# Loading the first column piece of w_down as two halves

## The chip, the core and the metric

The kernel runs on one core of a Trainium2 chip. It computes one decode step of a transformer block: conditioned layer norm, cached grouped-query attention over 65,536 positions, then a gated feed-forward layer. The metric is the device time of one execution in microseconds (us), of which lower is better. A profile is one execution taken by the hardware profiler; its span is about 1.4 us shorter than the timed figure of the same execution (437.0 against 438.43 us for the kernel before).

The engines are PE (TensorE, matmul; PEld is its weight load), DVE (VectorE), ACT (ScalarE), POOL (GpSimd), and SP, which here only issues DMAs.

## The reference, cut to what matters

The change touches only the very last product, the multiplication by `w_down` (3584 x 1024, bf16), and the sum with the residual:

```python
def _B_ref(x, w_gate, w_up, w_down):
    return _gelu(x @ w_gate) * (x @ w_up) @ w_down
...
h = _layernorm(x, axis=-1) * (1 + cb) + sb
x = x + gb * _B_ref(h, B_w_gate, B_w_up, B_w_down)
return x
```

There is one token, so every weight matrix is read once and used for a matrix-vector product. `w_down` is 7.3 MB of the 185.6 MB that the kernel reads from HBM.

## The kernel before

`w_down` is cut into seven blocks of 1 MB, numbered b = 0 to 6. A block holds four rows per partition (`UE = 4`), of 1024 columns (`D`). Blocks 0 to 4 are the row part, blocks 5 and 6 the column part.

```python
NBF = FD // UE          # 7
b = 0
NROW = NBF - 2          # 5: blocks 5 and 6 are multiplied column-wise
while b + 2 < NROW:     # blocks 0+1 and 2+3: 2 MB each
    ...
while b < NBF:
    for e, ne in ((0, UE),) if b + 1 < NBF else ((0, 2), (2, 1), (3, 1)):
        if b == NROW:   # block 5: beside block 4, in the same buffer
            jb = plan_load(
                wd_v[:, b, e:e + ne, :], flat(ne, D), jb.slot, beside=jb, off=UE * D, sem=9)
        else:
            jb = plan_load(wd_v[:, b, e:e + ne, :], flat(ne, D), next(tail_d))
        j_d.append((jb, jb.view, b * UE + e, ne))
    b += 1
```

So the last loads, in order, are 1 MB (block 4, the row piece), 1 MB (block 5), 512 KB, 256 KB and 256 KB (block 6). All go out on one queue; each has a semaphore that PE waits for.

The row part is multiplied with the activation as the stationary operand and the weights streaming past, and leaves partial sums along the rows of PSUM (`kt_ps` in the views). They must be turned into a column and added to the column part. The turn is two DVE transposes (L860), followed by eight small matmuls on PE, which I call the fold (L868; the program's four float32 matmuls show as eight). The column part takes the weights as the stationary operand, 128 columns at a time, with one activation column moving (L386): eight matmuls for each row of a block, so 32 for a block of 1 MB.

```python
early = [a for a in j_d if a[2] < NROW * UE]
v = row_matvec(place_d, early, o_pad, (v_uc,), (NQ - 1, NROW * UE - NQ))     # L409
DVE.wait(v)
for h in range(2):
    v_rows = DVE.done(dve.transpose(...))                                     # L860
late = j_d[len(early):]
col_matvec(acc_dn, late[:1], o_pad[:, :, 0], KD, True)                        # L386
PE.wait(v_rows, v_sel)
turned = row_a.rearrange("p (a k r) -> p a k r", a=NQ, r=QD)
for a in range(NQ):
    pe.matmul(acc_dn[QD * a:QD * (a + 1), :], sel32[:, :], turned[:, a, :, 0],
              start=False, stop=True, skip_group_check=True)                  # L868, the fold
v = col_matvec(acc_dn, late[1:], o_pad[:, :, 0], KD, False)                   # L386
DVE.wait(v)
v = DVE.done(dve.tensor_tensor(t_dn, acc_dn, mod_sb[:, 5, :], ALU.mult))      # L873
DVE.wait(v)
v = DVE.done(dve.tensor_tensor(y_col, t_dn, x1_col[:, :], ALU.add))           # L875
SP.wait(v)
sp.dma_start(out[0, 0].rearrange("(p k) -> p k", p=P), y_col)...              # L877
```

`late` is the list of column pieces. `late[:1]` is its first piece and `late[1:]` the rest. The fold stands between them, so the meaning of "first piece" decides where the fold stands. `col_matvec` waits for each piece's own semaphore in turn.

## Time and profile before

| Kernel before | |
|---|---|
| time | 438.57 us median (438.42 to 438.61, 6 runs) |
| span of the profiled execution | 437.0 us |
| read from HBM | 185.60 MB, 425 GB/s over the span |

The first view is the page's own slices, 40 equal ones over the span. The DMA line is the busy share in tenths, and the line under it is what the DMA engines moved.

```profile
DMA  8999999999999999999999999999999999999995
GB/s 359 432 425 441 433 430 427 439 425 438 435 432 432 433 432 432 432 435 432 432 438 432 432 433 432 432 432 432 432 432 432 432 427 435 439 432 433 420 422 229
```

The body of the kernel is a stream of loads that keeps the DMA engines at 8 or 9 tenths in every slice but the last, so I read its time as set by bytes. Only the last slice shows the DMA engines half idle: there the stream is over, and something else still runs. The next view is the chain of waits of the kernel before, in order of time: start, duration, what.

```profile
398.61 32.14 DMA slots<-in_B_w_down_dram
430.76 0.05 issue
430.80 2.09 PE b L386 x32
432.89 0.22 PE b L868 x8
433.11 2.03 PE b L386 x32
435.15 0.02 issue
435.17 0.18 DVE kt_sb L873
```

From 430.80 to 435.15 us the chain is PE work with no gap. The timeline of the same kernel tells what preceded it (start, duration, engine, line, operation; in brackets the idle time of the engine before it and what ended it).

```profile
428.35 1.05 PE L409 MATMUL kt_ps<-slots,p_row 128*32 128x512 bf16 x8 [0.51 <-DMA slots<-in_B_w_down_dram]
429.47 1.31 DVE L860 STREAM_TRANSPOSE kt_sb<-kt_ps 128x512 f32<-128x512 f32 x2 [7.69 <-PE kt_ps L409]
430.80 2.09 PE L386 MATMUL b<-p_row,slots 128*128 128x1 bf16 x32 [1.40 <-DMA slots<-in_B_w_down_dram]
432.82 0.29 PE L868 MATMUL b<-kt_sb,sel 128*32 128x8 f32 x8
433.05 2.09 PE L386 MATMUL b<-p_row,slots 128*128 128x1 bf16 x32
435.17 0.17 DVE L873 TENSOR_TENSOR kt_sb<-b,mod_sb 128x8 f32<-128x8 f32 x1 [4.39 <-PE b L386]
```

PE finishes the row part at 429.40 and then sits idle for 1.40 us until all of block 5 has landed. The second group of 32 follows the fold without a gap, so the pieces of block 6 were there in time.

A DMA's semaphore is counted up in 16 steps, and a load has landed at the last of them. Read so from the trace, in us from the span's start:

```
                 block 4   block 5   512 KB   256 KB   256 KB
kernel before     428.30    430.76   432.05   432.70   433.29
```

The data is complete at 433.29, but the last DVE product starts only at 435.17. PE is late because it began late.

### The profile page before, as it was taken

The page shows a single profiled execution, that of the slowest core. Times are in us where ns is not written, and L with a number is a line of the kernel's source. Part 1 is how long each engine was busy: PE and PEld are TensorE (multiplying, and loading weights), DVE is VectorE, ACT ScalarE, POOL GpSimd, SP SyncE. Part 2 cuts the span into 40 slices and gives each one's busy share as a digit, 9 for nine tenths or more (in the row PEclk, how much of TensorE's full clock was granted, in tenths as well). Part 3 has the DMA queues.
Part 4 walks back from the last instruction along what each step waited for, and adds up shares of the span by engine and source line. Part 5 has one row for each costly group of instructions (what it writes and reads, how often), then busy time and mean ns, then how long its engine had stood idle before and what let it go on. Part 6 is the DMA issues. An engine that isn't in the chain of part 4 may idle for free.

```text
span 437.0 us, 8422 instructions
## 1 busy us (share of the span) xinstructions
PE 306.8 (70%) x3858; PEld 201.2 (46%) x3858; DVE 206.7 (47%) x303; ACT 111.3 (25%) x164; POOL 16.8 (4%) x23
## 2 busy tenths in 40 slices
PE   0435459969697778959687895969778596575356
PEld 0112236646565555636465563646556363232024
DVE  6601014646474656737373763737476365321001
ACT  1000001533333513433241353333235334000000
POOL 9500000000000000000000000000000000000000
PEclk9986669988798978979696897879889879578685
DMA  8999999999999999999999999999999999999995
GB/s 359 432 425 441 433 430 427 439 425 438 435 432 432 433 432 432 432 435 432 432 438 432 432 433 432 432 432 432 432 432 432 432 427 435 439 432 433 420 422 229
DMA packets 8048, 185.77 MB, mean 425 GB/s; under 512 B 994, under 2 KB 994, under 8 KB 1380
## 3 DMA queue, kind: packets, MB, share of 16 engines
q1 hardware_dynamic: 8032, 185.60, 98.8%
q8 instruction: 8, 0.13, 0.1%
q14 instruction: 4, 0.03, 0.0%
q10 hardware_dynamic: 4, 0.00, 0.0%
HBM read 185.60 MB, written 0.00 MB: 425 GB/s over the span
## 4 chain that ended last, share of the span: by engine, by line
DMA 55%; PE 32%; DVE 10%; issue 1%; ACT 1%; POOL 0%; SPq 0%; POOLq 0%
DMA slots<-in_A_k_cache_dram 44%; PE kt_ps L575 16%; DMA slots<-in_B_w_down_dram 7%; PE b L645 5%; PE sc_ps L597 4%; DMA slots<-in_A_v_cache_dram 4%; PE kt_ps L409 4%; DVE selt L359 3%; DVE kt_sb L683 2%; DVE s_pad L717 1%; DVE o_red L706 1%; PE b L386 1%; PE sc_ps L626 1%; PE b L613 1%; DVE o_acc L694 1%
## 5 line engine op out<-in xcount | busy, mean ns | idle before, releaser
L575 PE MATMUL kt_ps<-ident,slots 128*128 128x128 bf16 x2048 | 157.6, 238 | 45.5 <-DMA slots<-in_A_k_cache_dram 44.7
L575 PEld LDWEIGHTS kt_ps<-ident,slots 128*128 128x128 bf16 x2048 | 136.9, 108 | 71.8 <-issue 41.0
L683 DVE COPY kt_sb<-kt_ps 128x2048 bf16<-128x2048 bf16 x96 | 117.6, 1225 | 109.5 <-PE kt_ps L575 107.8
L683 ACT ACTIVATE kt_sb<-kt_ps 128x2048 bf16<-128x2048 bf16 x32 | 60.1, 1878 | 28.0 <-PE kt_ps L575 28.0
L732 ACT ACTIVATE p_sb<-sc_ps 128x512 bf16<-128x512 bf16 x32 | 19.1, 598 | 181.6 <-PE sc_ps L626 181.6
L597 PE MATMUL sc_ps<-kt_sb,q_buf 128*32 128x512 bf16 x528 | 51.9, 428 | 0.0
L645 PE MATMUL b<-slots,p_sb 128*32 128x512 bf16 x560 | 42.0, 427 | 4.6 <-DMA slots<-in_A_v_cache_dram 3.9
L409 PE MATMUL kt_ps<-slots,h_pad 128*32 128x512 bf16 x176 | 19.4, 579 | 21.9 <-DMA slots<-in_A_wq_dram 9.5
L694 DVE SCALAR_TENSOR_TENSOR o_acc<-o_acc,s_pad,b 128x512 f32<-128x512 f32 x28 | 20.9, 747 | 13.5 <-PE b L645 13.4
L613 PE MATMUL b<-m_sp,selt 128*128 128x16 f32 x66 | 13.0, 272 | 18.1 <-DVE m_sp L722 16.5
L645 PEld LDWEIGHTS b<-slots,p_sb 128*32 128x32 bf16 x560 | 16.1, 108 | 20.7 <-issue 7.5
L717 DVE TENSOR_REDUCE s_pad<-sc_ps 128x1 f32<-128x512 f32 x32 | 21.8, 681 | 0.0
L738 ACT ACTIVATE p_row<-sc_ps,s_pad 128x512 bf16<-128x512 f32 x32 | 21.7, 678 | 0.0
L409 PEld LDWEIGHTS kt_ps<-slots,h_pad 128*32 128x32 bf16 x176 | 6.4, 129 | 32.7 <-issue 11.4
L613 PEld LDWEIGHTS b<-m_sp,selt 128*128 128x128 f32 x66 | 9.8, 188 | 23.7 <-DVE m_sp L722 21.3
L597 PEld LDWEIGHTS sc_ps<-kt_sb,q_buf 128*32 128x32 bf16 x528 | 11.0, 95 | 12.4 <-issue 4.7
L409 PE MATMUL kt_ps<-slots,s_pad 128*32 128x512 bf16 x96 | 11.6, 543 | 6.6 <-DMA slots<-in_w_mod_dram 6.6
L452 POOL TENSOR_TENSOR rs<-va,halfneg 128x1 f32<-128x1 f32 x2 | 1.1, 557 | 376.4 <-DVE va L449 376.4
L793 DVE COPY kt_sb<-kt_ps 128x512 f32<-128x512 f32 x3 | 2.1, 692 | 27.4 <-PE kt_ps L409 27.4
L626 PEld LDWEIGHTS sc_ps<-ident,p_row 128*128 128x128 bf16 x136 | 7.8, 99 | 15.1 <-issue 14.4
L626 PE MATMUL sc_ps<-ident,p_row 128*128 128x128 bf16 x136 | 13.7, 224 | 0.2 <-ACT p_row L738 0.2
L409 PE MATMUL kt_ps<-slots,p_row 128*32 128x512 bf16 x104 | 10.0, 543 | 4.4 <-DMA slots<-in_B_w_down_dram 3.6
(98 smaller groups left out, 142.8 us busy)
## 6 DMA issues: line engine op xcount, KB each, us to landing
slots<-in_A_k_cache_dram SPq DMA_DIRECT2D x16, 4096.0 KB, 23.1
slots<-in_A_v_cache_dram SPq DMA_DIRECT2D x16, 4096.0 KB, 23.2
slots<-in_w_mod_dram SPq DMA_DIRECT2D x4, 3072.0 KB, 20.3
slots<-in_A_wq_dram SPq DMA_DIRECT2D x2, 4096.0 KB, 35.3
slots<-in_A_wo_dram SPq DMA_DIRECT2D x4, 2048.0 KB, 24.6
slots<-in_B_w_gate_dram SPq DMA_DIRECT2D x2, 3584.0 KB, 29.5
slots<-in_B_w_up_dram SPq DMA_DIRECT2D x2, 3584.0 KB, 29.5
slots<-in_B_w_down_dram SPq DMA_DIRECT2D x2, 2048.0 KB, 34.4
```

The source lines that it names most:

```text
L359: dve.tensor_scalar(selt[:, :].rearrange("p (r h) -> p r h", h=REP), selw[:, HQ - REP:HQ].unsqueeze(1).to_broadcast([P, NR, REP]), -scale, ...
L409: ins = pe.matmul(out, pad[:, k, :], view[:, kk, c0:c0 + ROW], start=k <= last_k[0], stop=k >= last_k[1], skip_group_check=True,)
L575: ins = pe.transpose(kt_ps[:, half * 2048 + t * P:half * 2048 + (t + 1) * P], j_k[i - i % KU].view[:, i % KU * CH + b * TB + t, :], ident[ ...
L597: ins = pe.matmul(sc(j)[QD * g:QD * (g + 1), :], q_buf[:, j % SITES, QD * b:QD * (b + 1)], kt_sb[:, j % 2, n:n + w, :].rearrange("p n d -> ...
L613: ins = pe.matmul(b6[:, 0:NR], selt[:, :], m_sp[:, j % 2, :], start=True, stop=True)
L626: ins = pe.transpose(sc_bf[:, o:o + P], p_row[:, j % 2, c * P:(c + 1) * P], ident[:, :])
L645: ins = pe.matmul(b7[QD * c:QD * (c + 1), :].rearrange("p (b d) -> p b d", b=NB), p_sb[:, s, c * P + QD * g:c * P + QD * (g + 1)], v[:, NQ ...
L683: ev[i % SITES][b].done(act.activation(dst, src, ACT.Copy) if E_ is AC else dve.tensor_copy(dst, src))
L694: v = oc[j % SITES].done(dve.scalar_tensor_tensor(o_acc[:, :], o_acc[:, :], al[:, j:j + 1], b7[:, :], ALU.mult, ALU.add))
L717: v = DVE.done(dve.tensor_reduce(m_new, sc(j), AX.X, ALU.max))
L732: pc[jt % SITES].done(act.activation(p_sb[:, jt % SITES, :], sc_bf[:, o:o + ROW], ACT.Copy))
L738: v_x[j] = ex[s].done(act.activation(p_row[:, j % 2, :], sc(j), ACT.Exp, bias=mneg[:, j:j + 1], scale=scale, accum_out=zr[:, j:j + 1],))
```

## The change

The intent is to let PE start on block 5 when half of it is there. Each half gets a semaphore of its own (numbers 9 and 7), so that PE can wait for each half alone.

```diff
-            for e, ne in ((0, UE),) if b + 1 < NBF else ((0, 2), (2, 1), (3, 1)):
+            for e, ne in ((0, UE),) if b < NROW else ((0, 2), (2, 2)) if b == NROW else ((0, 2), (2, 1), (3, 1)):
                 if b == NROW:
                     jb = plan_load(
-                        wd_v[:, b, e:e + ne, :], flat(ne, D), jb.slot, beside=jb, off=UE * D, sem=9)
+                        wd_v[:, b, e:e + ne, :], flat(ne, D), jb.slot, beside=jb, off=(UE + e) * D, sem=9 - e)
```

Because `late[:1]` is now a half, the fold moves as well: PE's order is 16 column matmuls, fold, 48 column matmuls, in place of 32, fold, 32. No other instruction moves.

## The prediction

> **What bounds the kernel now.** The span is 437.0 us. The slices of the page show the DMA engines at 8 to 9 tenths nearly throughout, mostly at 432 GB/s, with 185.6 MB read: the body is a stream of loads, and the change leaves its bytes alone. What it can move is the tail. The chain of waits ends: DMA of w_down until 430.76; column matvec 2.09 us (32 matmuls); fold of the turned rows 0.22 us (L868); column matvec 2.03 us (32 matmuls, from 433.11); two DVE steps of 0.18 us; then the output store, issued at 435.57.
>
> By the semaphore updates in the trace, the last loads land at 428.30 (the piece before), 430.76 (the 1 MB piece), 432.05 (512 KB), 432.70 and 433.29 (256 KB each). PE idles 1.40 us for the 1 MB piece, and the remaining 4.4 us are PE work, though the last byte lands at 433.29 and needs only 8 matmuls, 60 ns apart.
>
> **What the change does.** It splits the 1 MB load into two of 512 KB, each waited for on its own. The fold now stands after the first half: 16 column matmuls, fold, 16, then 32, instead of 32, fold, 32. Matmuls and bytes are the same; one DMA issue (0.43 us on SP, far ahead of the data) and one semaphore wait are added.
>
> **Costs.** In this stream a 512 KB piece landed 1.29 us after its predecessor, where half of the 1 MB step would be 1.23 us. I estimate the first half to land at 429.55 to 429.6, the second near 430.85; later pieces shift by up to 0.1 us. The Trainium skill, "DMA: Bandwidth & Descriptors", section "Rules for kernel authors", advises at least 1 MiB per DMA for bandwidth; the 1.29 us (406 GB/s) of this trace says that the loss is small when loads are queued behind one another.
>
> **The critical path after.** PE starts at 429.6 and does 16 matmuls by 430.65. The fold needs the DVE transposes, which end at 430.78, so it starts near 430.83: a new wait of 0.1 to 0.2 us on DVE. Then 16 matmuls from 431.05 to 432.05, about when the 512 KB piece of the last block lands (432.1). From there 32 matmuls, 2.13 us to the DVE step as before (433.04 to 435.17): DVE starts near 434.25 rather than 435.17. The gain is about 0.9 of the 1.2 us by which the first half comes sooner; DVE and the 512 KB landing take the rest. The stream before 428 is untouched.
>
> Predicted time: 438.57 - 0.9 = 437.65 us, 8 in 10 between 437.0 and 438.4 (run-to-run scatter 0.2 us, some drift between chips). Faster by over 2%: 0.01; within 2%: 0.98; slower by over 2%: 0.01.
>
> **What would show it.** PE's idle time before the first column matmuls, put down to DMA, falls from 1.40 us to about 0.2. The fold is preceded by a wait on the DVE transpose (L860). The column matvecs run from 429.6 to 434.2. The last landing stays within 0.1 us of 433.29. The idle time before the DVE product L873 ends about 0.9 us sooner. The chain of waits turns to DVE L860 or the last 512 KB landing.
>
> **What would make it wrong.** Smaller pieces that cost the stream more than 0.1 us; landings of the halves bunched together, since the 16 engines finish one load over 1.85 us and the slowest sets its landing; a granted clock other than the 0.5 of this tail; SP blocked on a full queue (its last two issues took 5.7 and 6.6 us) for long enough to starve it.

## The result, and the profile after

| | before | after |
|---|---|---|
| time, median (range) of 6 runs each | 438.57 us (438.42 to 438.61) | 437.56 us (437.46 to 437.69) |
| ratio | | 0.9978, 95% interval 0.9965 to 0.9990 |
| span of the profiled execution | 437.0 us | 436.2 us |
| start of the DVE product L873 | 435.17 | 434.32 |

The ratio and its interval are given as recorded, from fast runs alone; the ratio of the medians quoted would be 0.9977. The change gains 1.01 us by the medians, 0.2% of the whole. The ranges of the two kernels do not overlap, though by a limit of 2% the two count as the same.

The chain of waits after the change, in order of time:

```profile
397.44 30.93 DMA slots<-in_B_w_down_dram
428.38 0.04 issue
428.42 1.10 PE kt_ps L409 x8
429.52 0.03 issue
429.55 1.33 DVE kt_sb L860 x2
430.87 0.04 issue
430.92 0.29 PE b L868 x8
431.21 3.09 PE b L386 x48
434.30 0.02 issue
434.32 0.18 DVE kt_sb L873
```

The load that the chain hangs on is now block 4, landing at 428.38, and no longer block 5. Between it and PE's last stretch stand the row matmuls and the DVE transposes. The timeline after the change shows the former idle time in use:

```profile
429.55 1.31 DVE L860 STREAM_TRANSPOSE kt_sb<-kt_ps 128x512 f32<-128x512 f32 x2 [6.81 <-PE kt_ps L409]
429.67 1.13 PE L386 MATMUL b<-p_row,slots 128*128 128x1 bf16 x16 [0.19 <-DMA slots<-in_B_w_down_dram]
430.91 0.20 PEld L868 LDWEIGHTS b<-kt_sb,sel 128*32 128x32 f32 x8 [0.20 <-DVE kt_sb L860]
430.92 0.29 PE L868 MATMUL b<-kt_sb,sel 128*32 128x8 f32 x8
431.14 3.14 PE L386 MATMUL b<-p_row,slots 128*128 128x1 bf16 x48
434.32 0.17 DVE L873 TENSOR_TENSOR kt_sb<-b,mod_sb 128x8 f32<-128x8 f32 x1 [3.46 <-PE b L386]
```

PE's wait of 1.40 us for block 5 has become 0.19 us for its first half and 0.20 us (on the weight load) for the transposes. Sixteen column matmuls run while DVE transposes. After the fold there are 48, not 32, but they start at 431.14 rather than 433.05.

The landings after the change:

```
                 block 4   1st half   2nd half   512 KB   256 KB   256 KB
kernel after      428.38     429.62     430.89   432.13   432.76   433.40
```

The last byte lands 4.99 us after block 4 before the change (433.29 - 428.30) and 5.02 us after it now (433.40 - 428.38). The extra DMA cost the stream about 0.03 us. The rest of the shift, 0.08 us, was there when block 4 landed, ahead of anything that the change touched on the queue; the profiled executions below scatter by about 0.3 us at that point. I therefore compare profiles by the time from the landing of block 4 to the start of the DVE product. It is 6.87 us before (435.17 - 428.30) and 5.94 us after (434.32 - 428.38), 0.93 us less.

### The profile page after: what moved, and what is told of

Read it like the earlier page. It is cut to its first block, busy times and chain, and to the rows that moved or that the text cites. A ratio compares the mean times of both kernels' runs of the same rounds, so it can differ in the third digit from the quotient of the medians.

```text
span 436.2 us, 8423 instructions
## 1 busy us (share of the span) xinstructions
PE 302.8 (69%) x3858; PEld 200.5 (46%) x3858; DVE 206.7 (47%) x303; ACT 111.2 (26%) x164; POOL 16.8 (4%) x23
## 4 chain that ended last, share of the span: by engine, by line
DMA 56%; PE 31%; DVE 11%; issue 1%; ACT 1%; POOL 0%; POOLq 0%
DMA slots<-in_A_k_cache_dram 45%; PE kt_ps L575 16%; DMA slots<-in_B_w_down_dram 7%; PE b L645 4%; DMA slots<-in_A_v_cache_dram 4%; PE sc_ps L597 4%; PE kt_ps L409 3%; DVE selt L359 3%; DVE kt_sb L683 2%; DVE s_pad L717 1%; DVE o_red L706 1%; PE sc_ps L626 1%; PE b L613 1%; PE b L386 1%; DVE o_acc L694 1%
## 5 line engine op out<-in xcount | busy, mean ns | idle before, releaser
L597 PE MATMUL sc_ps<-kt_sb,q_buf 128*32 128x512 bf16 x528 | 50.8, 420 | 0.0
L645 PE MATMUL b<-slots,p_sb 128*32 128x512 bf16 x560 | 40.1, 411 | 5.3 <-DMA slots<-in_A_v_cache_dram 4.6
L727 DVE TENSOR_REDUCE s_pad<-b 128x1 f32<-128x16 f32 x32 | 5.6, 175 | 14.6 <-PE b L613 14.6
```

The lines of the kernel that those rows point to most:

```text
L597: ins = pe.matmul(sc(j)[QD * g:QD * (g + 1), :], q_buf[:, j % SITES, QD * b:QD * (b + 1)], kt_sb[:, j % 2, n:n + w, :].rearrange("p n d -> ...
L645: ins = pe.matmul(b7[QD * c:QD * (c + 1), :].rearrange("p (b d) -> p b d", b=NB), p_sb[:, s, c * P + QD * g:c * P + QD * (g + 1)], v[:, NQ ...
```

## The experiments

My theory, called M, is that the gain is nothing but column matmuls that PE does in time in which it used to idle, with the fold and the landings as the limits. The rivals are S (the smaller loads make the stream or its landings faster by themselves), F (the fold's earlier place makes the gain), E (the earlier the first landing, the larger the gain) and, for a later run, L (the end is bound by the landing of the 512 KB piece).

The table has all eleven runs, five timed executions each, with the median of the kernel before (nine executions), and from each profile the two intervals that matter, both counted from the landing of block 4 (its second half, where it is loaded in two). Intervals are differences of times rounded to 0.01 us. Each of the three calls ran on a chip of its own; the kernel before took 438.49, 438.57 and 438.50 us on them.

| run | median us (range) | before | to DVE product | to last landing |
|---|---|---|---|---|
| split_one_wait | 438.62 (438.42 to 438.65) | 438.49 | 6.95 | 5.02 |
| split_fold_late | 437.69 (437.59 to 437.76) | 438.49 | 5.99 | 5.01 |
| whole_fold_first | 438.42 (438.25 to 438.54) | 438.49 | 6.81 | 4.98 |
| after_again | 437.56 (437.48 to 437.66) | 438.49 | 5.94 | 5.02 |
| split_768_256 | 437.94 (437.75 to 437.98) | 438.57 | 6.29 | 5.02 |
| split_256_768 | 438.03 (437.93 to 438.04) | 438.57 | 6.34 | 5.02 |
| four_pieces | 437.70 (437.58 to 437.89) | 438.57 | 6.01 | 5.16 |
| four_and_four | 437.54 (437.48 to 437.65) | 438.57 | 5.89 | 5.15 |
| two_and_four | 437.52 (437.45 to 437.59) | 438.50 | 5.87 | 5.07 |
| row_two_and_four | 437.46 (437.39 to 437.48) | 438.50 | 5.85 | 5.11 |
| after_third | 437.51 (437.34 to 437.63) | 438.50 | 5.97 | 5.03 |

All gave correct results. The edits below are against the changed kernel unless said otherwise.

### Two halves, one wait

```diff
+        PE.wait(late[1][0].tok)
-        col_matvec(acc_dn, late[:1], o_pad[:, :, 0], KD, True)
+        col_matvec(acc_dn, late[:2], o_pad[:, :, 0], KD, True)
 ...
-        v = col_matvec(acc_dn, late[1:], o_pad[:, :, 0], KD, False)
+        v = col_matvec(acc_dn, late[2:], o_pad[:, :, 0], KD, False)
```

> Both halves are loaded as in the changed kernel, but PE waits for both before the first column matmul, and the fold stands after all 32 again. Theory M (the gain is the 16 column matmuls that PE now does while it used to idle for the 1 MB piece): the gain is gone; matmuls start near 430.9, DVE product near 435.2 to 435.3, time 438.5 to 438.7. Rival S (the two smaller loads themselves make the stream or its landings faster): 437.5 to 437.7 stays. The last landing stays at 433.3 to 433.4 under M.

It took 438.62 us: the gain is gone, with the same loads. The timeline of this run:

```profile
430.88 2.09 PE L386 MATMUL b<-p_row,slots 128*128 128x1 bf16 x32 [1.47 <-DMA slots<-in_B_w_down_dram]
432.90 0.29 PE L869 MATMUL b<-kt_sb,sel 128*32 128x8 f32 x8
433.13 2.10 PE L386 MATMUL b<-p_row,slots 128*128 128x1 bf16 x32
```

The idle time before the first column matmul is back, at 1.47 us. That is the picture of the kernel before, 0.08 us later because the second half lands 2.53 us after block 4 where the whole block landed 2.46 us after it. Rival S falls: the smaller loads gain nothing by themselves.

### Two halves, fold after the second

```diff
-        col_matvec(acc_dn, late[:1], o_pad[:, :, 0], KD, True)
+        col_matvec(acc_dn, late[:2], o_pad[:, :, 0], KD, True)
 ...
-        v = col_matvec(acc_dn, late[1:], o_pad[:, :, 0], KD, False)
+        v = col_matvec(acc_dn, late[2:], o_pad[:, :, 0], KD, False)
```

> Two loads with a wait each, but the fold stands after the second half (32 matmuls, fold, 32). Theory M: the first 16 still run in the former idle time, the second 16 wait for the landing near 430.9 where the fold waited for DVE before, so the time is that of the changed kernel within 0.1 us: 437.5 to 437.7. Rival F (the gain comes from the fold standing earlier, in an idle time of PE): 438.4 to 438.6.

It took 437.69 us, 0.80 us less than the kernel before. The timeline:

```profile
429.76 2.42 PE L386 MATMUL b<-p_row,slots 128*128 128x1 bf16 x32 [0.19 <-DMA slots<-in_B_w_down_dram]
431.02 1.07 PEld L386 LDWEIGHTS b<-p_row,slots 128*128 128x128 bf16 x16 [0.21 <-DMA slots<-in_B_w_down_dram]
432.10 0.30 PE L868 MATMUL b<-kt_sb,sel 128*32 128x8 f32 x8
```

The fold is in its old place, after 32 matmuls, and most of the gain stays: the first 16 matmuls run in the former idle time, and the second 16 wait for the second half where the fold waited for DVE. So F falls as the cause of the gain. The time is 0.13 us above the control (437.56 us). From block 4 to the DVE product the profiles differ by 0.05 us, and that small rest I leave unexplained.

### One load, fold first

This edit is made in the kernel before: the first `col_matvec` is dropped, the fold starts the accumulation, and all column pieces follow it.

```diff
-        col_matvec(acc_dn, late[:1], o_pad[:, :, 0], KD, True)
 ...
-                start=False, stop=True, skip_group_check=True)
+                start=True, stop=True, skip_group_check=True)
-        v = col_matvec(acc_dn, late[1:], o_pad[:, :, 0], KD, False)
+        v = col_matvec(acc_dn, late, o_pad[:, :, 0], KD, False)
```

> One 1 MB load as in the kernel before, but the fold stands before all column matmuls. Theory M: the fold needs the DVE transposes, which end at 430.8, the same moment as the 1 MB landing, so nothing is hidden: 438.4 to 438.6 (up to 0.1 us less from one switch less on PE). Rival F (the fold's place makes the gain): 437.6 to 437.9.

It took 438.42 us, as the kernel before within its scatter (438.49). The timeline:

```profile
430.90 0.30 PE L867 MATMUL b<-kt_sb,sel 128*32 128x8 f32 x8 [1.44 <-DVE kt_sb L860]
431.13 4.01 PE L386 MATMUL b<-p_row,slots 128*128 128x1 bf16 x64
```

PE idles 1.44 us all the same, only the name of what it waits for has changed. Before the change, two waits ended within 0.1 us of each other: the landing of block 5 (430.82 in this run) and the end of the transposes. Moving the fold alone cannot help, because the fold itself is not ready earlier. The work that is ready is the column matmuls of the first half, and it takes the split load to make it so.

### Uneven splits

```diff
-((0, 2), (2, 2)) if b == NROW
+((0, 3), (3, 1)) if b == NROW        # split_768_256
+((0, 1), (1, 3)) if b == NROW        # split_256_768
```

This diff and those of the next runs are cut to the list of pieces. The semaphores stay 9 and 7, and the fold stays after the first piece.

> Pieces of 768 KB and 256 KB, fold after the first. Theory M counts the column matmuls that are done before the DVE transposes end near 430.9: the first piece lands near 430.25, so about 10 of 24 are hidden and the fold runs at 431.7; DVE product near 434.65, time 437.8 to 438.0. Rival S (any split in two speeds the stream alike): 437.5 to 437.7.

> Pieces of 256 KB and 768 KB, fold after the first. First landing near 429.05, before PE is free at 429.5. Theory M: only 8 matmuls are hidden, 56 follow the fold at 430.9: DVE product near 434.75, time 437.9 to 438.1, slower than the even split although its first piece lands first. Rival E (the earlier the first landing, the larger the gain): 437.4 or less. Rival S: 437.5 to 437.7.

They took 437.94 and 438.03 us, 0.63 and 0.54 us less than the kernel before; both fall in the ranges that M gave. The timeline of the 768 KB first run:

```profile
430.41 1.61 PE L386 MATMUL b<-p_row,slots 128*128 128x1 bf16 x24 [0.80 <-DMA slots<-in_B_w_down_dram]
431.95 0.29 PE L868 MATMUL b<-kt_sb,sel 128*32 128x8 f32 x8
432.18 2.58 PE L386 MATMUL b<-p_row,slots 128*128 128x1 bf16 x40
```

And of the 256 KB first run:

```profile
429.47 0.66 PE L386 MATMUL b<-p_row,slots 128*128 128x1 bf16 x8
430.97 0.30 PE L868 MATMUL b<-kt_sb,sel 128*32 128x8 f32 x8 [0.84 <-DVE kt_sb L860]
431.20 3.54 PE L386 MATMUL b<-p_row,slots 128*128 128x1 bf16 x56
```

With 768 KB first, PE starts late (0.80 us idle). With 256 KB first, it starts at once but has only eight matmuls to do, and then waits 0.84 us for the transposes. What counts is how many column matmuls are done when the fold could start. With 768 KB first the transposes end at 430.99, so the fold could start near 431.05 (in the changed kernel it starts about 0.06 us after their end). By then about ten are done (0.64 us from 430.41, at 60 ns from one start to the next in the trace), as M expected; with 256 KB first it is eight, and in the even split 16. The missing six and eight are 0.36 and 0.48 us. From block 4 to the DVE product the two lose 0.35 and 0.40 us against the control (6.29 and 6.34 against 5.94). It was run on another chip. The gains over the kernel before are 0.30 and 0.39 us smaller than the control's 0.93. Rival E falls with the second of them, and S once more with both.

### Four pieces, and four in the last block too

```diff
-((0, 2), (2, 2)) if b == NROW else ((0, 2), (2, 1), (3, 1)):
+((0, 1), (1, 1), (2, 1), (3, 1)) if b == NROW else ((0, 2), (2, 1), (3, 1)):            # four_pieces
+((0, 1), (1, 1), (2, 1), (3, 1)) if b == NROW else ((0, 1), (1, 1), (2, 1), (3, 1)):    # four_and_four
```

In both, the fold stands after the third piece, and each added piece has a semaphore of its own. The second 256 KB of the last block lies beside the first in its buffer.

> The block as four pieces of 256 KB, fold after the third. Theory M: 24 matmuls run from 429.5 to 431.0, fold, 8 more until 431.8, then PE waits about 0.4 us for the 512 KB piece of the last block (landing 432.15 to 432.25): DVE product 434.3 to 434.4, time 437.5 to 437.7, no gain over two pieces, because the wait for that landing takes it. If two more DMAs cost the stream more than 0.1 us, slower: 437.8. Without the landing's limit it would be 437.1.

> As four_pieces, and the last block also as four pieces of 256 KB rather than 512, 256, 256. Theory M: the 0.4 us wait is filled, and the last 8 matmuls follow the last landing (433.4 to 433.55): DVE product near 434.15, time 437.3 to 437.5, the fastest of all, and bound by the last landing. If the smaller pieces cost the stream 0.2 us or more in all: 437.6 or slower.

The first took 437.70 us, at the upper end of what M expected. The timeline:

```profile
429.65 1.64 PE L386 MATMUL b<-p_row,slots 128*128 128x1 bf16 x24
431.23 0.30 PE L868 MATMUL b<-kt_sb,sel 128*32 128x8 f32 x8
431.45 0.66 PE L386 MATMUL b<-p_row,slots 128*128 128x1 bf16 x8
432.50 2.10 PE L386 MATMUL b<-p_row,slots 128*128 128x1 bf16 x32 [0.39 <-DMA slots<-in_B_w_down_dram]
```

PE does 24 matmuls before the fold and the fold waits for nothing, yet the lead is lost in a new wait of 0.39 us for the 512 KB piece. M had put that wait at about 0.4 us.

The second run fills that wait, and took 437.54 us, where I had expected 437.3 to 437.5: a near miss. In its profile the last piece landed at 433.76, not by 433.55 as expected, and the DVE product started 0.74 us after it (434.50). Of the lateness, 0.23 us was in the stream already at block 4 (428.61 against 428.38), which other profiles show too, and 0.13 us is the cost of three more pieces (5.15 us from block 4 to the last landing, against 5.02). The 0.17 us that the added overlap should have brought (434.32 - 434.15) went mostly to that cost. Smaller pieces are cheap here but not free: by the last column of the table each added piece costs 0.04 to 0.07 us in these two runs.

### The last block alone, and the row piece split as well

`two_and_four` keeps the two halves and cuts block 6 into four. `row_two_and_four` does so and also loads block 4, the row piece, as two halves.

```diff
-((0, UE),) if b < NROW else ((0, 2), (2, 2)) if b == NROW else ((0, 2), (2, 1), (3, 1)):
+((0, UE),) if b < NROW else ((0, 2), (2, 2)) if b == NROW else ((0, 1), (1, 1), (2, 1), (3, 1)):         # two_and_four
+((0, 2), (2, 2)) if b < NROW else ((0, 2), (2, 2)) if b == NROW else ((0, 1), (1, 1), (2, 1), (3, 1)):   # row_two_and_four
```

> The changed kernel with its last block in four pieces of 256 KB rather than 512, 256, 256. Theory M: PE works without a gap from the fold at 430.9 to the end, and waits for none of these landings by more than 0.05 us, so nothing is gained: DVE product near 434.3, time 437.5 to 437.7. Rival L (the end is bound by the landing of the 512 KB piece): 437.3 to 437.45.

> As two_and_four, and the row block before (the 1 MB piece that lands at 428.3) also as two halves, so that its last row matmuls end about 0.5 us sooner and the DVE transposes end near 430.35. Theory M: the fold then waits for no DVE, the 0.2 us wait ahead of it goes; PE reaches the last landing (433.45 to 433.6) about when it comes, and 8 matmuls follow it: DVE product near 434.2, time 437.35 to 437.6, at most 0.2 us better than the changed kernel. If the DMA pieces cost the stream 0.1 us or more, no better than it.

The first took 437.52 us, and its control (the changed kernel) 437.51 us. By the times, rival L is not supported. Its limits lie only 0.07 us away, less than the scatter, so the control rather than the expected range decides. The timeline of the first:

```profile
431.11 0.30 PE L871 MATMUL b<-kt_sb,sel 128*32 128x8 f32 x8
431.34 3.06 PE L389 MATMUL b<-p_row,slots 128*128 128x1 bf16 x48
434.44 0.17 DVE L876 TENSOR_TENSOR kt_sb<-b,mod_sb 128x8 f32<-128x8 f32 x1 [3.38 <-PE b L389]
```

The profiles do show a small term. In the changed kernel PE stops briefly at the landing of the 512 KB piece (432.13): the next matmul starts 95 ns after the one before it, not 60, and with the slower starts that follow, eight intervals take 0.56 us, not 0.48. In `two_and_four` that stop is gone (48 matmuls last 3.06 us, not 3.14), and block 4 to the DVE product is 0.07 to 0.10 us less than in the three profiles of the changed kernel (5.87 against 5.94, 5.94 and 5.97). So this landing costs the changed kernel about 0.1 us at most, which the times do not resolve. The second took 437.46 us (437.39 to 437.48), inside the range of its control (437.34 to 437.63). Its timeline:

```profile
428.52 0.61 PE L415 MATMUL kt_ps<-slots,p_row 128*32 128x512 bf16 x4 [0.64 <-DMA slots<-in_B_w_down_dram]
429.18 1.31 DVE L866 STREAM_TRANSPOSE kt_sb<-kt_ps 128x512 f32<-128x512 f32 x2 [6.40 <-PE kt_ps L415]
429.81 1.14 PE L392 MATMUL b<-p_row,slots 128*128 128x1 bf16 x16 [0.68 <-DMA slots<-in_B_w_down_dram]
430.89 0.25 PE L874 MATMUL b<-kt_sb,sel 128*32 128x8 f32 x8
431.07 3.22 PE L392 MATMUL b<-p_row,slots 128*128 128x1 bf16 x48
```

The transposes end at 430.49 here, and the fold no longer waits for them. (The fold was also shorter, by about 0.04 us: in this profile the granted clock was 1.00 until 431.09 us, in all the others 0.50 from 428.3 us on.) But the DVE product starts at 434.33, 0.74 us after the last landing (433.59), just as in `four_and_four`. In the changed kernel that distance is 0.92 us (434.32 - 433.40). In the trace of both runs PE does wait for the last landing: its last eight matmuls start 0.05 us after it, 169 ns after the matmul before them here and 139 ns in `four_and_four`, where 60 is usual. I read this as the next limit: the last 256 KB and the eight matmuls that need it. It is a near one: in `row_two_and_four` PE waits only 0.11 us there, and its work already fills the rest of the time from the landing of the first half of block 5 (429.77). No run removed this limit, so it is read from the two traces and not shown by an experiment. No version tried beats the changed kernel by more than the scatter.

### The changed kernel again

> The changed kernel again, as a control beside the three others: 437.5 to 437.7 under every theory.

> The changed kernel again on the same chip as these two, as a control: 437.5 to 437.7.

The controls took 437.56 and 437.51 us, 0.93 and 0.99 us less than the kernel before of their calls. With the first measurement (1.01 us), the gain is about 1.0 us.

## Why the prediction was right

- **What bounds the kernel.** The prediction held that the body is bound by bytes and only the tail can move. The body did not move: the timed gain of about 1.0 us is matched by the 0.93 us between block 4 and the DVE product.
- **The mechanism.** It said that PE's idle time of 1.40 us would fall to about 0.2 us and that 16 matmuls would run in it. It fell to 0.19 us. `split_one_wait` puts the idle time back, with the same loads, and the gain is gone.
- **The new small wait on DVE.** The fold was predicted to start near 430.83 after a wait of 0.1 to 0.2 us. It started at 430.92 after 0.20 us, and the chain of waits now runs through L860, as predicted.
- **The landings.** The first half was put at 429.55 to 429.6 and the second near 430.85; they landed at 429.62 and 430.89. The last landing was to stay within 0.1 us of 433.29 and came at 433.40, so it missed that by 0.01 us. Of the lateness of each, 0.08 us was there before block 5.
- **The end.** The DVE product was put near 434.25 and started at 434.32. The predicted gain was 0.9 us, the measured one 1.01 us, and the predicted time 437.65 us against 437.56 us. The stated range, 437.0 to 438.4 us, was wide enough for a gain of 0.2 us as well as one of 1.6 us; the time alone would have proved little, and it is the points in the trace that bear the prediction out.
- **A cost that was put too high.** The step for a 512 KB piece was taken as 1.29 us from the one example in the trace. The three of the changed kernel took 1.24, 1.27 and 1.24 us.
- **What took the rest.** From the landing of block 4 the first half came 1.22 us sooner than the whole block had (1.24 against 2.46 us), and the gain was 0.93 us. The prediction gave the rest to DVE and the 512 KB landing. The start of the fold, held up by DVE, took about 0.19 us (316 ns from the matmul before it, not the 128 ns of the kernel before), and the 512 KB landing about 0.08 us.
- **What was feared and did not come.** The Trainium skill, "DMA: Bandwidth & Descriptors", section "Rules for kernel authors", advises at least 1 MiB per DMA. In this stream half of that cost about 0.03 us. Single issues on SP did take long, and longer than before: in the changed kernel that of a 512 KB load took 7.37 us, where the longest of the kernel before took 6.62 us. Yet its last issue ended at 415.95, and that load landed at 433.40, so the load was queued long before it landed. The granted clock was 0.50 in the whole tail of both kernels (from 428 us on), so it explains no difference.

## What to carry to other kernels

When a kernel ends in a compute tail behind a saturated stream of loads, look for the engine that idles for one large load just before the tail, and split that load so that work which needs only part of it fills the idle time. Size the piece by what else gates the tail: here the DVE transposes were ready about 1.4 us after PE came free, so half a block (16 matmuls, 1.0 us) fitted, while a quarter gave too little work and three quarters came too late. Stop when the next limit is the last landing plus the work that needs it, because more pieces then only add cost to the stream.

## What the Trainium skill lacked or had wrong

- "Perfetto Trace Analysis", section "DMA Optimizations", says that splitting a DMA may let work start sooner and names the case of DMA engines that are generally idle. Here they were busy (407 GB/s from 429.5 to 431.0 us, in both kernels), and the split still gained about 1.0 us, since what it filled was PE's idle time.
- "DMA: Bandwidth & Descriptors", section "Rules for kernel authors", advises at least 1 MiB per DMA and does not say what less costs when loads are queued behind one another. In the changed kernel 512 KB pieces landed 1.24 to 1.27 us apart (413 to 423 GB/s, the size over that time), and the 1 MB piece of the kernel before 2.46 us after its predecessor (426 GB/s).
- "Perfetto Trace Analysis", section 'What "DMA-bound" means', reads a solid run of DMA slices on the issuing sequencer as a limit by that sequencer. In the changed kernel SP issued almost without a gap from 397.44 to 415.95 us, single issues taking up to 7.37 us, while the loads so issued landed 17 us and more after the end of their issue, in a stream that moved 420 GB/s (424 to 428 us). The stream was not short of issues. I read the long ones as SP waiting for room in the queue; no run tested that.
- No page that I read gives a figure for how far apart the 16 semaphore steps of one load come in a long stream. In the kernel before, the 16 semaphore steps of block 5 came between 428.91 and 430.76 us, eight by 429.67 and eight from 430.50 on. The first k_cache load of the same execution shows 1.7 us, loads around 200 us 1.9 us, and the first w_mod load 0.9 us, so the distance arose early and stayed. What causes it was not tested. It bears on this tail, since a piece counts as landed only at the last of its steps.
- "TensorE: Matmul & The Clock Gate", section "Back-to-back issue gap", gives for small matmuls an issue floor of about 25 ns, or about 62 ns with hardware decode off. The column matmuls here (128 weight columns, one moving column) started mostly 60 ns apart, at a granted clock of 0.50 (the changed kernel, from 429.65 us) and at 1.00 (`row_two_and_four`, 429.80 to 430.90 us) alike. That is close to the page's second figure and does not follow the clock. But each of these matmuls comes with a weight load of its own, and no run here varied either that or the decode, so what sets the 60 ns stays open.
